# kv products of the second block on high and low parts of G and wv

## The chip, the core and the metric

One core of a Trainium2 chip runs the whole program. The metric is the device time of one execution in microseconds (us), the median of several runs. The core has a matrix engine (TensorE, PE in the profile, with its weight loads as PEld), three engines for element-wise work (VectorE or DVE, ScalarE or ACT, GpSimd or POOL) and SyncE (SP), which here only issues transfers. Each takes its instructions strictly in the order of the program. Matrix products read from SBUF and write to PSUM; the other engines take results out of PSUM.

## The reference

Two independent linear-attention blocks, A and B, on inputs of the same shape; the outputs stand side by side. For each of them, with S = 2048 tokens, D = 640, H = 32 heads of Dh = 20:

```python
qkv = (x @ wqkv).reshape(B, S, 3, H, Dh).transpose(2, 0, 3, 1, 4)
q, k, v = qkv[0], qkv[1], qkv[2]
phi = lambda t: jnp.where(t > 0, t + 1, jnp.exp(t)) + 1e-6
pq, pk = phi(q), phi(k)
kv = jnp.einsum("bhsd,bhse->bhde", pk, v)
z = jnp.einsum("bhsd->bhd", pk)
num = jnp.einsum("bhqd,bhde->bhqe", pq, kv)
den = jnp.einsum("bhqd,bhd->bhq", pq, z)[..., None] + 1e-6
o = num / den
out = o.transpose(0, 2, 1, 3).reshape(B, S, D) @ wo
```

All of it is float32.

## The kernel before

Large products aren't done in float32. Each operand is split into a high part, rounded to the type float32r (ScalarE copies, `ACTIVATE`), and a low part, the operand less the high part (VectorE, `TENSOR_TENSOR`), and three products high x high, high x low, low x high stand in for one (`mms`, `mm3`). In the second half of the kernel the helper `split` (lines 917 to 921) issues the ScalarE copy at once and only notes the subtraction in the list `lows`; `flush` issues what is noted, and `run` calls `flush` ahead of the work of its slot. So a low part stands on VectorE behind everything that was written between the `split` and the next slot.

v is never formed. With G = x^T phi(k), a 640 x 640 matrix, kv of a group of heads is wv^T G, cut to the heads' own blocks by a mask; then M = kv wo, folded over all heads, is one 640 x 640 matrix for each block, and the output is (phi(q) / den) M. The stages, in order of time:

- k stage: phi(k) for both blocks and G, summed up in five SBUF tiles `gacc` (one for each 128 rows c). A planner (`Plan`) orders this half by costs and due times. The last rounds of G of block B end it (psg, line 316; the sums on VectorE, line 537).
- q stages and output stages, written out by hand: q(0), q(1), out(0), q(2), out(1), ... up to out(7); u = 0 to 3 are tokens of block A, 4 to 7 of block B. A q stage (`qmm`) has five column pieces c, and for each five products k of three matrix instructions (lines 924 to 926), 512 columns wide, into the PSUM tile psq; then `qphi` takes psq through exp and relu on ScalarE (lines 1092, 1093) and one VectorE instruction (line 1094). psq rotates over three banks. An output stage (`outmm`) has 14 steps; ScalarE copies pa out (line 1249), VectorE adds pe and psb (line 1250).

Everything else is hung on slots: `at(("q", u, c, k), f, ...)` runs f right after product k of piece c of stage q(u), `at(("o", u, s), ...)` after step s of out(u). In the slots of q(0) stand the kv products of block B: `kvmm2(1, g)`, line 977, for six groups of heads g (four of 6 heads with 120 columns, two of 4 heads with 80), five products each over c, in float32: the 30 instructions show as 60 in the profile, each as two passes. The operands are `gacc[1, c]` and the loaded `wvt[1, g]`. Their slots are the pieces and products (0,2), (1,0), (1,3), (2,0), (2,3), (3,0).

Three more things around them matter later. `form_load` (line 1054) brings the split M of block A back from DRAM in ten pairs of transfers into tiles fh and fl; the first six have slots in q(0) and q(1), and go out on SyncE's queue. `load_xq` (line 957) brings the low parts xql of the next q stage, on the same queue, at ("q", 0, 3, 3) and ("q", 0, 4, 0) to ("q", 0, 4, 3). And `chain` (lines 1343 to 1365) spreads the sum over heads that makes the denominator (`fold1` to `fold5`, with ScalarE copies and VectorE sums) over the steps of the output stage before: for v = 1 they stand at steps 3, 4, 5, 6, 7, 9 and 11 of out(0).

Of the kernel before, what the change touches and what calls it, by code (L numbers as in the profile page):

```python
# [9 lines left out]
F32R = mybir.dt.float32r  # L10
# [4 lines left out]
H = 32  # L15
DH = 20
EPS = 1e-6
GROUPS = [(0, 6), (6, 6), (12, 6), (18, 6), (24, 4), (28, 4)]
# [200 lines left out]
def tile_linear_attn_pair(ctx: ExitStack, tc: tile.TileContext, ins, out: bass.AP):  # L219
    nc = tc.nc  # L220
    P = 128
    S, D = ins[0]["x"].shape
    NC = D // P
# [17 lines left out]
    kx, kg, q1a, q1b, q2, q3 = [], [], [], [], [], []  # L241
# [24 lines left out]
    gacc = {}  # L266
# [385 lines left out]
    wl, wh = ([Space(n, D, (XD,), F32R) for _ in range(NC)] for n in ("wkl", "wkh"))  # L652
# [16 lines left out]
    def whalf(h, *t):  # L669
        return [x[0][h * HF:h * HF + HF] for x in t]  # L670
# [6 lines left out]
    a, z, x = jh[0][0:P], jl[0][0:P], jr[0][0:P]  # L677
# [22 lines left out]
    for h in range(2):  # L700
        hi, lo = whalf(h, wh, wl)
# [79 lines left out]
    def filled(i, h, where=(1, 3, 4, 5, 6)):  # L781
        fill = {}
        for c, n in enumerate(where):
            fill.setdefault(n, []).append((gstep, i, h, c))
        return fill
# [9 lines left out]
    for p in range(4, NPB):  # L795
        i, h = divmod(p - 2, 2)
# [9 lines left out]
    for p in range(NPB + 1, NP):  # L806
        if p == NPB + 1:
            fl = kvs
        else:
            i, h = divmod(p - NPB - 2, 2)  # L810
            gready(NG + i)
            fl = filled(NG + i, h, *((LAST,) if p in (NPB + 2, NP - 1) else ()))
# [26 lines left out]
    wst, whl, wvt, xt, xts = {}, {}, {}, {}, {}  # L839
# [5 lines left out]
    def late(pool, name, cols, bufs):  # L845
        s = Late(name, cols, None, F32R)
        s.pool = pool
        s.make = lambda: s.open([P, cols], F32R, name=name, tag=name, bufs=bufs)
        return s

    for c in range(NC):
        hi, lo, raw = late(q1b, "wh", D, 5), late(q1b, "wl", D, 5), Space("wq", D, ANY)
# [13 lines left out]
    for c in range(NC):  # L866
        hi, lo, raw = late(q1b, "xqh", 512, 6), late(q1b, "xql", 512, 6), Space("xqs", 512, ANY)
# [13 lines left out]
    for g, (h0, nh) in enumerate(GROUPS):  # L881
        cols = NC * DH * nh
        w = Space("wv", cols, (BD,))
# [17 lines left out]
    def bank(name, tag="one", bufs=3):  # L901
        at, n = ptags[tag]
        pn[tag] = pn.get(tag, -1) + 1
        return psum.tile([P, 512], F32, name=name, tag=f"bank{at + pn[tag] % n}", bufs=1)

    def turned(tag, n):
        turn[tag] = (turn.get(tag, -1) + 1) % n
        return f"{tag}{places[turn[tag]] if tag == 'wst' else turn[tag]}"
# [3 lines left out]
    def flush():  # L912
        while lows:
            lo, src, hi = lows.pop(0)
            nc.vector.tensor_tensor(lo, src, f32(hi), op=OP.subtract)

    def split(hi, lo, src, now=False):
        nc.scalar.activation(hi, src, AF.Copy)  # L918
        lows.append((lo, src, hi))
        if now:  # L920
            flush()

    def mm3(o, whi, wlo, xhi, xlo, first, last):
        nc.tensor.matmul(o, whi, xhi, start=first, stop=False)  # L924
        nc.tensor.matmul(o, whi, xlo, start=False, stop=False)  # L925
        nc.tensor.matmul(o, wlo, xhi, start=False, stop=last)  # L926
# [3 lines left out]
    def at(slot, f, *a):  # L930
        todo.setdefault(slot, []).append((f, a))
# [34 lines left out]
    def load_o(b, g):  # L966
# [7 lines left out]
        nc.sync.dma_start(o, ins[b]["wo"][h0 * DH:(h0 + nh) * DH, :])  # L974
        wot[b, g] = o

    def kvmm2(b, g):
        h0, nh = GROUPS[g]
        r = DH * nh
        w = wvt.pop((b, g))  # L980
        ps = bank("pskv", "e", 2)
        for c in range(NC):
            gd = gacc[b, c].rearrange("p (d h) -> p d h", h=H)[:, :, h0:h0 + nh]
            nc.tensor.matmul(ps[:r, :r].rearrange("p (d h) -> p d h", h=nh), w[:, c, :], gd,
                             start=(c == 0), stop=(c == NC - 1))
        t = base.tile([r, r], F32, name="kvt", tag="kvt0", bufs=1)
        hi, lo = (base.tile([r, r], F32R, name=f"kv{t}", tag=turned("kvs", 12), bufs=1) for t in "hl")
        nc.vector.tensor_tensor(t, ps[:r, :r], mask[nh][:r, :], op=OP.mult)
        split(hi, lo, t)
        kvt[b, g] = (hi, lo)  # L990
# [79 lines left out]
    pq, acc, den, dd = {}, {}, {}, {}  # L1070
# [222 lines left out]
            at(s, form_store, b, i)  # L1293

    for i in range(6):
        at((("q", 0, 2, 1), ("q", 0, 2, 4), ("q", 0, 3, 1), ("q", 1, 0, 0), ("q", 1, 0, 2), ("q", 1, 1, 0))[i],
           form_load, 0, i)
    for i in range(6, 10):
        at(("q", 1, i - 5, 4) if i < 9 else ("q", 1, 4, 0), form_load, 0, i)

    for g in range(NGR):
        at(("q", 0, 0, 0), load_o, 1, g)
        at(("q", 0, (0, 1, 1, 2, 2, 3)[g], (2, 0, 3, 0, 3, 0)[g]), kvmm2, 1, g)
        at(("q", 0, 1 + g, 1) if g < 4 else ("q", 1, 0, 2 * g - 7), split_o, 1, g)
        at((("q", 0, 2, 2), ("q", 0, 3, 2), ("q", 0, 4, 4), ("q", 0, 4, 4), ("q", 1, 1, 2), ("q", 1, 2, 2))[g], mmm2, 1, g)
        at((("q", 0, 2, 4), ("q", 0, 3, 4), ("q", 1, 0, 1), ("q", 1, 0, 3), ("q", 1, 1, 4), ("q", 1, 2, 4))[g],
           store_m, nc.gpsimd)

    for c, a in ((0, ("q", 1, 4, 1)), (2, ("q", 1, 4, 1)), (4, ("q", 2, 0, 3)), (1, ("q", 4, 0, 2)), (3, ("q", 4, 0, 2))):
        at(a, load_w, "m", 1, c)  # L1310
    at(("o", 0, 5), form_sums1, 1, 0)
# [9 lines left out]
    h = NG - 1  # L1321
# [26 lines left out]
    for v in range(1, NU):  # L1348
        w, u = v - 1, v + 1
        if v == NU - 1:  # L1350
            chain[v] = [(("o", w, 1), split_acc, v), (("o", w, 4), denmm, v), (("o", w, 4), recip, v, 0),
                        (("o", w, 5), divide, v, 0), (("o", w, 6), a_split, v, 0, 0), (("o", w, 6), d_sums, v, 0, 0),
                        (("o", w, 7), d_split, v, 0, 0), (("o", w, 8), a_split, v, 1, 0), (("o", w, 8), d_sums, v, 1, 0),
                        (("o", w, 9), recip, v, 1), (("o", w, 10), d_split, v, 1, 0), (("o", w, 12), divide, v, 1),
                        (("o", v, 0), a_split, v, 0, 1), (("o", w, 13), d_sums, v, 0, 1),
                        (("o", v, 0), d_split, v, 0, 1), (("o", v, 2), d_sums, v, 1, 1),
                        (("o", v, 2), a_split, v, 1, 1), (("o", v, 3), d_split, v, 1, 1)]
        else:
            a = (3, 4, 5, 6, 7, 9, 11) if v == 1 else (2, 3, 5, 6, 7, 9, 11)
            chain[v] = [(("o", w, a[0]), fold1, v), (("o", w, a[1]), fold2, v), (("o", w, a[2]), fold3, v, 0),  # L1360
                        (("o", w, a[3]), fold3, v, 1), (("o", w, a[4]), fold4, v), (("o", w, a[5]), fold5, v, 0),
                        (("o", w, a[6]), fold5, v, 1), (("o", w, 11), divide, v, 0), (("o", w, 12), divide, v, 1),
                        (("q", u, 0, 2), d_sums, v, 0), (("q", u, 0, 4), a_split, v, 0), (("q", u, 1, 2), d_sums, v, 1),
                        (("q", u, 2, 1), d_split, v, 0), (("q", u, 3, 1), a_split, v, 1),
                        (("q", u, 3, 4), d_split, v, 1)]
# [66 lines left out]
```

## Time and profile before

| | before |
|---|---|
| median of 3 runs | 569.47 us (569.34 to 569.63) |
| the profiled execution | 570.12 us |
| its span on the core | 568.3 us |
| mean granted TensorE clock | 0.999 |
| busy: PE / PEld / DVE / ACT / POOL | 561.9 / 533.4 / 429.0 / 363.6 / 62.9 us |
| q(0) and q(1), with kv and M of block B | 287.49 to 333.47 us |
| out(0) | 333.47 to 351.09 us |
| moved by DMA | 117.64 MB, mean 207 GB/s |

The span is the time between the first and the last recorded instruction; the 1.8 us between it and the execution's time lie outside the program's instructions. Matrix instructions are pipelined: the recorded duration of one (0.39 us for 512 columns) is longer than the distance to the next (0.23 us), so distances between starts say what one costs. The time before an instruction that its engine stood idle is printed with what ended it. In views of stretches (windows) each engine has its busy time and number of instructions, then the TensorE clock that was granted, the share of the DMA engines and GB/s.

### The profile page before, as it was taken

What the parts mean: (1) busy time and instruction counts of PE and PEld (TensorE: products, weight loads), DVE (VectorE), ACT (ScalarE), POOL (GpSimd) and SP (SyncE); (2) the same over time, 40 slices, a digit from 0 to 9 for tenths busy, and PEclk for the clock granted to TensorE, in tenths of its full rate; (3) what the DMA queues carried; (4) which work ended last, traced back from release to release, by engine and by line L of the source; (5) the groups of instructions that cost most, each with busy time, mean ns of one, the idle gap of its engine ahead of it and who ended that gap; (6) DMA issues with size and microseconds to landing.
All of it is one profiled execution on the core that took longest, in us unless ns stands there. A gap on an engine that the chain in (4) does not pass through costs nothing. (4 is left out here: it accounts for less than half of the span.)

```text
span 568.3 us, 9523 instructions
## 1 busy us (share of the span) xinstructions
PE 561.9 (99%) x3512; PEld 533.4 (94%) x3512; DVE 429.0 (75%) x712; ACT 363.6 (64%) x673; POOL 62.9 (11%) x103
## 2 busy tenths in 40 slices
PE   8999999999999999999999999999999999999997
PEld 6999999999999999999988898898989989898997
DVE  6788677599888757988745798867788685767792
ACT  6778566574688756666446668675767666665551
POOL 0210111110001021110010103110012201001010
PEclk9999999999999999999999999999999999999999
DMA  8994664758849767696999975663373997122022
GB/s 292 358 293 122 177 167 104 243 150 236 273 122 265 197 169 197 190 295 202 340 294 337 357 255 175 250 229 120 101 247 119 349 389 264 47 76 92 1 93 92
DMA packets 68321, 117.64 MB, mean 207 GB/s; under 512 B 6804, under 2 KB 30132, under 8 KB 68276
## 3 DMA queue, kind: packets, MB, share of 16 engines
q1 hardware_dynamic: 59060, 89.94, 48.1%
q0 software_dynamic: 8928, 26.92, 17.1%
q8 instruction: 27, 0.44, 0.3%
q10 hardware_dynamic: 288, 0.20, 0.1%
q14 instruction: 18, 0.15, 0.1%
HBM read 71.13 MB, written 35.41 MB: 187 GB/s over the span
## 5 line engine op out<-in xcount | busy, mean ns | idle before, releaser
L316 PE MATMUL psg<-pkl,xnh 128*128 128x320 f32 x320 | 98.9, 309 | 0.0
L316 PE MATMUL psg<-pkh,xnh 128*128 128x320 f32 x320 | 98.8, 309 | 0.0
L316 PE MATMUL psg<-pkh,xnl 128*128 128x320 f32 x320 | 98.5, 308 | 0.0
L924 PE MATMUL psq<-xqh,wh 128*128 128x512 f32 x200 | 78.4, 392 | 0.0
L926 PE MATMUL psq<-xqh,wl 128*128 128x512 f32 x200 | 78.0, 390 | 0.0
L925 PE MATMUL psq<-xql,wh 128*128 128x512 f32 x200 | 77.9, 389 | 0.0
L489 ACT ACTIVATE kt<-ka 128x320 f32<-128x320 f32 x52 | 22.7, 437 | 59.1 <-PE ka L316 59.0
L316 PEld LDWEIGHTS psg<-pkl,xnh 128*128 128x128 f32 x320 | 60.1, 188 | 0.0
L316 PEld LDWEIGHTS psg<-pkh,xnl 128*128 128x128 f32 x320 | 60.1, 188 | 0.0
L316 PEld LDWEIGHTS psg<-pkh,xnh 128*128 128x128 f32 x320 | 60.0, 188 | 0.0
L406 POOL DMA_DIRECT2D zacc<-ek x32 | 26.5, 840 | 236.9 <-DVE ek L499 176.9
L1094 DVE SCALAR_TENSOR_TENSOR pq<-eq,rq 128x512 f32<-128x512 f32 x40 | 27.6, 691 | 32.1 <-ACT rq L1093 32.0
L1092 ACT ACTIVATE eq<-psq 128x512 f32<-128x512 f32 x40 | 23.9, 597 | 38.2 <-PE psq L926 35.9
L537 DVE TENSOR_TENSOR gacc<-psg,gacc 128x320 f32<-128x320 f32 x60 | 29.4, 490 | 23.7 <-PE psg L316 22.7
L926 PEld LDWEIGHTS psq<-xqh,wl 128*128 128x128 f32 x200 | 37.5, 188 | 7.9
L925 PEld LDWEIGHTS psq<-xql,wh 128*128 128x128 f32 x200 | 37.6, 188 | 7.3
L924 PEld LDWEIGHTS psq<-xqh,wh 128*128 128x128 f32 x200 | 37.6, 188 | 7.2
L1249 ACT ACTIVATE o<-pa 128x320 f32<-128x320 f32 x64 | 27.8, 437 | 25.6 <-PE pa L1234 25.1
L1234 PE MATMUL pa<-fh,dah 128*128 128x320 f32 x96 | 29.7, 310 | 1.4 <-ACT o L1249 1.4
L401 ACT ACTIVATE pkh<-ek,epst 128x640 fp32r<-128x640 f32 x32 | 26.5, 828 | 6.9 <-DVE ek L499 6.7
L1234 PE MATMUL pa<-fl,dah 128*128 128x320 f32 x96 | 29.7, 309 | 0.0
L1234 PE MATMUL pa<-fh,dal 128*128 128x320 f32 x96 | 29.6, 309 | 0.0
(222 smaller groups left out, 1564.4 us busy)
## 6 DMA issues: line engine op xcount, KB each, us to landing
zacc<-ek POOLq DMA_DIRECT2D x32, 320.0 KB, 4.8
xql<-xd SPq DMA_DIRECT2D x40, 256.0 KB, 4.9
xd<-xl SPq DMA_DIRECT2D x29, 320.0 KB, 4.3
out<-o POOLq DMA_DIRECT2D x28, 320.0 KB, 3.8
xns<-in_A_x SPq DMA_DIRECT2D x16, 320.0 KB, 5.5
xts<-in_B_xt_tiles SPq DMA_DIRECT2D x16, 320.0 KB, 3.7
xns<-in_B_x SPq DMA_DIRECT2D x16, 320.0 KB, 6.0
xqs<-in_A_xt SPq DMA_DIRECT2D x20, 256.0 KB, 5.6
```

Source lines behind the costliest of these rows:

```text
L316: nc.tensor.matmul(o, a.r, w.r, start=start and k == i == 0, stop=k == n - 1 and i == 2, skip_group_check=True)
L401: note("ACT", n + 110, lambda: act(hi.r, p.f, AF.Identity, bias=epst), [hi], [p, K0.all], by=8.0)
L406: note("POOL", 1.0, lambda: nc.gpsimd.dma_start(z.f, p.f, **kw), [z], [p], dma=1.0 if first else 1.86)
L489: note("ACT", HF, lambda: act(o.f, BK[k].tile[:, :HF], AF.Copy), [o], [BK[k].all])
L537: tt(o, BK[k].tile[:, :HF], o, op=OP.add)
L924: nc.tensor.matmul(o, whi, xhi, start=first, stop=False)
L925: nc.tensor.matmul(o, whi, xlo, start=False, stop=False)
L926: nc.tensor.matmul(o, wlo, xhi, start=False, stop=last)
L1092: nc.scalar.activation(e, ps, AF.Exp)
L1094: nc.vector.scalar_tensor_tensor(pq[u][:, c, :], e, 1.0, r, op0=OP.min, op1=OP.add)
L1234: nc.tensor.matmul(ps, x, y, start=start and n == i == 0, stop=n == len(terms) - 1 and i == 2, skip_group_check=True)
L1249: copy = lambda x, y: nc.scalar.activation(x, y, AF.Copy)
```

## The change

The kv products of block B get split operands. `gsplit(c)` makes a high part gh and a low part gl of `gacc[1, c]` (five of 640 columns), `vsplit(g)` a high part wvh and a low part wvl of the loaded wv of a group (four of 600 columns, two of 400). `kvmm2` then runs three float32r products in place of one float32 product: 90 instructions for 30. The new tiles lie in SBUF places of q tiles and of fh and fl that are free at that time, and the slots of `kvmm2` move back by two or three products, the first three `form_load`s move behind them, and the fold chain of v = 1 starts two steps later.

```diff
+    gs = {}
+
+    def gsplit(c):
+
+        if c == 0:
+            gs["all"] = q2[0].tile([P, NC, 512], F32R, name="gh", tag="pq", bufs=2).rearrange("p c s -> p (c s)")
+        g = gacc[1, c]
+        hi = gs["all"][:, c * D:c * D + D] if c < 4 else q2[0].tile([P, D], F32R, name="gh", tag="dah0", bufs=1)
+        lo = q1a[0].tile([P, D], F32R, name="gl", tag="fl", bufs=6)
+        split(hi, lo, g)
+        gs[c] = hi, lo
+
+    def vsplit(g):
+        w = wvt[1, g].rearrange("p c e -> p (c e)")
+        cols = NC * DH * GROUPS[g][1]
+        hi, lo = (q1a[0].tile([P, D], F32R, name=f"wv{t}", tag="fh", bufs=6)[:, :cols] for t in "hl")
+        split(hi, lo, w)
+        wvt[1, g] = [t.rearrange("p (c e) -> p c e", c=NC) for t in (hi, lo)]
+
     def kvmm2(b, g):
...
-        w = wvt.pop((b, g))
+        wh, wl = wvt.pop((b, g))
         ps = bank("pskv", "e", 2)
+        o = ps[:r, :r].rearrange("p (d h) -> p d h", h=nh)
         for c in range(NC):
-            gd = gacc[b, c].rearrange("p (d h) -> p d h", h=H)[:, :, h0:h0 + nh]
-            nc.tensor.matmul(ps[:r, :r].rearrange("p (d h) -> p d h", h=nh), w[:, c, :], gd,
-                             start=(c == 0), stop=(c == NC - 1))
+            gh, gl = (t.rearrange("p (d h) -> p d h", h=H)[:, :, h0:h0 + nh] for t in gs[c])
+            mm3(o, wh[:, c, :], wl[:, c, :], gh, gl, c == 0, c == NC - 1)
...
     for i in range(6):
-        at((("q", 0, 2, 1), ("q", 0, 2, 4), ("q", 0, 3, 1), ("q", 1, 0, 0), ("q", 1, 0, 2), ("q", 1, 1, 0))[i],
+        at((("q", 0, 3, 4), ("q", 0, 4, 1), ("q", 0, 4, 3), ("q", 1, 0, 0), ("q", 1, 0, 2), ("q", 1, 1, 0))[i],
            form_load, 0, i)
...
+    for c in range(NC):
+        at(("q", 0, 0, max(0, c - 1)), gsplit, c)
     for g in range(NGR):
         at(("q", 0, 0, 0), load_o, 1, g)
-        at(("q", 0, (0, 1, 1, 2, 2, 3)[g], (2, 0, 3, 0, 3, 0)[g]), kvmm2, 1, g)
+        at(("q", 0, (1, 1, 2, 2, 3, 3)[g], (0, 3, 0, 3, 0, 3)[g]), kvmm2, 1, g)
...
+    for g, a in enumerate((("q", 0, 0, 4), ("q", 0, 0, 4), ("q", 0, 0, 4), ("q", 0, 1, 3), ("q", 0, 2, 0), ("q", 0, 2, 3))):
+        at(a, vsplit, g)
...
-            a = (3, 4, 5, 6, 7, 9, 11) if v == 1 else (2, 3, 5, 6, 7, 9, 11)
+            a = (5, 6, 7, 7, 8, 10, 11) if v == 1 else (2, 3, 5, 6, 7, 9, 11)
```

Where the changed program puts these instructions shows in three places. The first is VectorE's list at the start of q(0). zsum, zturn and zp belong to the sums z over phi(k); kvt and kvl come out of a finished kv group, pq out of a finished column piece of q. Before:

```order
L602 STREAM_TRANSPOSE zturn<-zsum 128x640
L603 TENSOR_REDUCE zp<-zturn 128x5x4
L988 TENSOR_TENSOR kvt<-pskv,mask_74 120x120
L915 TENSOR_TENSOR kvl<-kvt,kvh 120x120
L1094 SCALAR_TENSOR_TENSOR pq<-eq,rq 128x512
```

And in the changed program:

```order
L602 STREAM_TRANSPOSE zturn<-zsum 128x640
L603 TENSOR_REDUCE zp<-zturn 128x5x4
L915 TENSOR_TENSOR gl<-gacc,gh 128x640 x5
L1113 SCALAR_TENSOR_TENSOR pq<-eq,rq 128x512
L915 TENSOR_TENSOR wvl<-wv,wvh 128x600 x3
L1007 TENSOR_TENSOR kvt<-pskv,mask_74 120x120
L915 TENSOR_TENSOR kvl<-kvt,kvh 120x120
```

All five gl and the first pq now stand ahead of the first wvl. On TensorE the first kv group follows the 18th matrix instruction of q(0) (before: the ninth), and its own third instruction reads that wvl:

```order
L924 MATMUL psq<-xqh,wh 128x512
L925 MATMUL psq<-xql,wh 128x512
L926 MATMUL psq<-xqh,wl 128x512
L924 MATMUL pskv<-gh,wvh 120x120
L925 MATMUL pskv<-gl,wvh 120x120
L926 MATMUL pskv<-gh,wvl 120x120
```

The second place is SyncE's list near the end of q(0): xqs and xql are the next stage's operands, fh and fl the pairs of `form_load`. Before:

```order
L955 DMA xqs<-in_A_xt 128x512 x4
L1068 DMA fh<-fdh_96 128x640
L1068 DMA fl<-fdl_97 128x640
L955 DMA xqs<-in_A_xt 128x512
L1068 DMA fh<-fdh_98 128x640
L1068 DMA fl<-fdl_99 128x640
L1068 DMA fh<-fdh_100 128x640
L1068 DMA fl<-fdl_101 128x640
L959 DMA xql<-xd_85 128x512 x5
```

And in the changed program:

```order
L955 DMA xqs<-in_A_xt 128x512 x5
L959 DMA xql<-xd_85 128x512
L1087 DMA fh<-fdh_96 128x640
L1087 DMA fl<-fdl_97 128x640
L959 DMA xql<-xd_85 128x512
L1087 DMA fh<-fdh_98 128x640
L1087 DMA fl<-fdl_99 128x640
L959 DMA xql<-xd_85 128x512 x2
L1087 DMA fh<-fdh_100 128x640
L1087 DMA fl<-fdl_101 128x640
L959 DMA xql<-xd_85 128x512
```

Two pairs of fh and fl now stand between the second and the last xql. The third place is ScalarE's list in out(0): o is the copy of pa out of PSUM, ac the fold chain's copies, xqh and fsh high parts of other operands. Before:

```order
L1249 ACTIVATE o<-pa 128x320 x2
L1126 ACTIVATE ac<-acc 64x256
L1127 ACTIVATE ac<-acc 64x256
L1249 ACTIVATE o<-pa 128x320
L962 ACTIVATE xqh<-xqs 128x512
L1249 ACTIVATE o<-pa 128x320
L1140 ACTIVATE ac<-ac 32x256 x2
L962 ACTIVATE xqh<-xqs 128x512
L1140 ACTIVATE ac<-ac 32x256 x2
L918 ACTIVATE fsh<-wst 128x640
L1249 ACTIVATE o<-pa 128x320
```

And in the changed program:

```order
L1268 ACTIVATE o<-pa 128x320 x3
L962 ACTIVATE xqh<-xqs 128x512
L1268 ACTIVATE o<-pa 128x320
L1145 ACTIVATE ac<-acc 64x256
L1146 ACTIVATE ac<-acc 64x256
L962 ACTIVATE xqh<-xqs 128x512
L918 ACTIVATE fsh<-wst 128x640
L1159 ACTIVATE ac<-ac 32x256 x4
L1268 ACTIVATE o<-pa 128x320
```

Four output copies come ahead of the first fold copy now, two before, and the four later fold copies stand in one row ahead of the fifth.

## The prediction

> **What bounds the kernel now.** The page's busy times come first:
>
> ```profile
> PE 561.9 (99%) x3512; PEld 533.4 (94%) x3512; DVE 429.0 (75%) x712; ACT 363.6 (64%) x673; POOL 62.9 (11%) x103
> ```
>
> TensorE is busy for 99% of the span. A busy TensorE need not be at its peak, so the stages that the change touches are read by stretches. The columns are the stretch and its length, then for PE, PEld, DVE, ACT and POOL the busy time with the number of instructions, then the granted TensorE clock, the DMA share and GB/s.
>
> ```profile
> 287.49:333.47 45.98, 45.98 (x250) 39.28 (x249) 31.17 (x51) 26.78 (x53) 6.42 (x11) 1.00 0.96 318
> 333.47:351.09 17.62, 16.25 (x110) 15.86 (x108) 16.03 (x25) 13.81 (x30) 2.57 (x5) 1.00 0.51 161
> 368.12:383.96 15.84, 15.84 (x109) 15.84 (x108) 10.68 (x17) 11.75 (x26) 3.03 (x6) 1.00 0.69 243
> ```
>
> The first stretch is q(0) and q(1), the second out(0), the third out(1). In the q stages TensorE never waits: what is added to its list, and each new wait, goes straight into the time. VectorE (31 of 46 us) and ScalarE (27) have room on average, which says nothing of one moment. out(0) has the same products as out(1) and takes 1.78 us more: that is the only time nearby that can be won back.
>
> **Term 1, the products: +2.8 us.** The timeline of TensorE and its weight loads around two kv groups (start, length, engine, line, count):
>
> ```profile
> 289.34 0.39 PE L926 MATMUL psq<-xqh,wl 128*128 128x512 f32 x1
> 289.57 1.21 PE L984 MATMUL pskv<-gacc,wv 128*120 128x120 f32 x10
> 290.51 0.19 PEld L924 LDWEIGHTS psq<-xqh,wh 128*128 128x128 f32 x1
> 290.54 0.47 PE L924 MATMUL psq<-xqh,wh 128*128 128x512 f32 x1
> 290.63 0.19 PEld L925 LDWEIGHTS psq<-xql,wh 128*128 128x128 f32 x1
> 290.86 0.39 PE L925 MATMUL psq<-xql,wh 128*128 128x512 f32 x1
> 302.30 0.88 PE L984 MATMUL pskv<-gacc,wv 128*80 128x80 f32 x10
> 302.95 0.19 PEld L924 LDWEIGHTS psq<-xqh,wh 128*128 128x128 f32 x1
> ```
>
> Five float32 products are ten passes. A weight load starts with the instruction ahead of its own, so the load at 290.51 marks the tenth pass: (290.51 - 289.57) / 9 = 0.104 us a pass at 120 columns, (302.95 - 302.30) / 9 = 0.072 at 80. That is the distance of weight loads too: the 128-column load of 290.51 lets the next one start at 290.63, and the instruction of 290.54 is followed only at 290.86, 0.32 us on, where 512 columns otherwise take 0.23. It stood until its weights were in. So a short product goes as fast as weights load, some 0.11 us for 128 columns, 0.104 for 120, 0.072 for 80. A float32r product loads as many weight columns and is one pass; no row shows one narrower than 320. Taken at the pace of the weights, a group has 15 in place of 10: 5 x 0.104 = 0.52 us, 5 x 0.072 = 0.36; 4 x 0.52 + 2 x 0.36 = **+2.8**. Bounds: 512 columns take 0.23 and 320 take 0.147,
>
> ```profile
> 343.87 0.31 PE L1234 MATMUL pa<-fl,dah 128*128 128x320 f32 x1
> 344.02 0.31 PE L1234 MATMUL pa<-fh,dal 128*128 128x320 f32 x1
> ```
>
> so 0.43 ns a column and a line through 0.06 us at 120 and 0.04 at 80: 15 x 0.06 = 0.9 in place of 1.04, and -0.5 for all six groups if columns alone counted. Above, a narrow float32r product at the price of both float32 passes, 0.21 and 0.14: 15 x 0.21 - 1.04 = 2.1, and 1.4, so +11.2. I stay with the weights, the nearest row.
>
> [...]
>
> **Term 2, a wait for the first wvl: +4.0 us.** VectorE's list at the start of q(0), and rows for what the change puts into it:
>
> ```profile
> 289.89 0.82 DVE L603 TENSOR_REDUCE zp<-zturn 128x20 f32<-128x640 f32 x1
> 281.06 1.55 DVE L861 TENSOR_TENSOR wl<-wq,wh 128x640 fp32r<-128x640 f32 x2
> 293.39 0.69 DVE L1094 SCALAR_TENSOR_TENSOR pq<-eq,rq 128x512 f32<-128x512 f32 x1 [1.63 <-ACT rq L1093]
> 294.00 0.28 DVE L988 TENSOR_TENSOR kvt<-pskv,mask 120x120 f32<-120x120 f32 x1
> 278.48 1.98 ACT L857 ACTIVATE wh<-wq 128x640 fp32r<-128x640 f32 x3
> 292.27 0.60 ACT L1092 ACTIVATE eq<-psq 128x512 f32<-128x512 f32 x1 [0.83 <-PE psq L926]
> 292.76 0.59 ACT L1093 ACTIVATE rq<-psq 128x512 f32<-128x512 f32 x1
> ```
>
> zp ends at 290.7. Then come five gl; wl is the same operation and size, two in 1.55 us, 0.73 apart: until 294.35. Then pq, which hands on after 0.61 (293.39 to 294.00): 294.96. Then the first wvl, 600 columns, 0.78: **295.75**, and the signal. ScalarE's part is no later: its gh start once the last G products have left the place that they take, about 287.6; five at 0.63 (wh: three in 1.98) and three wvh at 0.6 end near 292.6, then eq and rq until 293.7, ahead of pq's turn at 294.35. TensorE reaches the first kv group after 18 instructions of 0.23 us, 287.49 + 4.14 = 291.63, runs two products, and wants wvl at 291.84. It waits 295.8 - 291.84 = **4.0 us**. Queued behind is all of TensorE's list, which nothing reorders, so the wait is paid whole. The later wvl have three or more products of cover each, 2 us against 0.8, and cost nothing. Bounds: 3.4 if VectorE hands on faster, 4.6 if pq has to wait for rq; 0 only if that list were not in the way at all.
>
> **Term 3, the clock: +1.2 us.** Rows for what a wait does to TensorE's clock:
>
> ```profile
> 345.70 0.41 PE L1234 MATMUL pa<-fh,dah 128*128 128x320 f32 x1 [1.37 <-ACT o L1249]
> 564.49 0.31 PE L1234 MATMUL pe<-fh,dal 128*128 128x320 f32 x1
> 567.00:567.60 0.60, 0.00 (x0) 0.00 (x0) 0.00 (x0) 0.00 (x0) 0.00 (x0) 1.00 0.00 0
> 567.60:568.30 0.70, 0.00 (x0) 0.00 (x0) 0.00 (x0) 0.00 (x0) 0.00 (x0) 0.52 0.00 0
> L647 PE MATMUL psi<-idle 128*128 128x512 bf16 x10 | 4.0, 581 | 1.0 <-DVE ones L324 1.0
> ```
>
> The 1.4 us idle of 344 left the clock at 1.00 (stretch rows above). The last product starts at 564.49, and from 567.6, 3.1 us on, the clock is about half. A wait of 4.0 us is longer than that. At the start ten 512-column products take 4.0 us, 0.4 each against 0.23 later: after some 4 us of work the clock is up. If it falls about 3 us into the wait, one more microsecond of its up-time passes in the wait, and some 2.4 us of work go at half speed, which loses **1.2 us**. Bounds: 0, if it doesn't fall; 2.1, if it falls at the wait's end and 4.2 us go slowly.
>
> [...]
>
> **Term 4, xql behind the fh and fl pairs: +0.4 us.**
>
> ```profile
> 309.48 2.36 SPq L959 DMA_DIRECT2D xql<-xd  x4
> 316.97 0.39 PE L925 MATMUL psq<-xql,wh 128*128 128x512 f32 x1
> xql<-xd SPq DMA_DIRECT2D x40, 256.0 KB, 4.9
> 294.00:327.00 33.00, 33.00 (x182) 28.27 (x181) 20.67 (x35) 20.80 (x43) 5.84 (x10) 1.00 1.03 336
> ```
>
> The last four xql can't go out before TensorE has read the old ones, in the last column piece of q(0); they go 309.48 to 311.8, the last lands after 4.9 us at about 316.4, and q(1) wants it at 316.97. With two pairs between them, 1.28 MB more lie ahead of it, 3.8 us at 336 GB/s, less the 0.5 us of margin: +3.3 at worst. But the queue is emptier by then: the first pair, which now goes ahead of that point, has had 7 us (the added time) to land, and the old order had three pairs there. Nearer to nothing, I take 0.4; lower bound 0.
>
> **Term 5, the fold chain: -1.0 us.**
>
> ```profile
> 343.72 0.84 ACT L1140 ACTIVATE ac<-ac 32x256 f32<-32x256 f32 x2
> 344.58 0.74 ACT L918 ACTIVATE fsh<-wst 128x640 fp32r<-128x640 f32 x1
> 345.23 0.42 ACT L1249 ACTIVATE o<-pa 128x320 f32<-128x320 f32 x1
> ```
>
> TensorE's 1.4 us idle at 345.70 ends with the copy of 345.23, which stood behind two fold copies and fsh. In the new order four output copies come ahead of the fold chain, but four fold copies (4 x 0.33 = 1.3 us) then stand in a row before the fifth. Between all of the 1.78 and nothing I take -1.0.
>
> **No cost:** the added high and low parts, 11 on ScalarE (about 7.6 us by the rows above) and 11 on VectorE (8.3), lie beside TensorE's work after the first group; without that cover each would cost what term 2 shows. The form pairs are wanted in out(0), 16 us and more after their new slots.
>
> **Sum:** 2.8 + 4.0 + 1.2 + 0.4 - 1.0 = +7.4. The profiled execution took 570.12 us (span 568.3 and 1.8 around it) and would take 577.5; the median, 0.65 lower, goes from 569.47 to **576.9**.
>
> **Rivals.**
> - The clock stays up: term 3 is 0, 575.7. For it speaks that a wait of 4.0 us is not much over 3.1; against it the end of the trace. 30%.
> - Narrow float32r products cost both passes: term 1 is 11.2, 585.3. For it: no row shows one below 320 columns; against it: one pass for each wide one. 9%.
> - Narrow products go by columns: term 1 is -0.5, 573.6. Against it is the product held up for its weights at 290.54. 7%.
> - The wait is hidden, VectorE gets to wvl before TensorE: terms 2 and 3 are 0, 571.7. Against it is the order. 4%.
> - Not slower: the fold chain is the one mechanism with a minus sign. It can give back 1.78 us in out(0), and decides only where everything else comes to less; with no wait and products by columns the time is 569.47 - 0.5 + 0.4 - 1.78 = 567.6. Or the products aren't changed as said. 3%.
>
> **How the numbers follow.** The forecast has 47%. 573.3 to 578.6 takes in the first rival, the third, and the spread of terms 2 to 5 upward, and leaves out the second, the fourth and the last, 16%. About 0.2% (1.1 us) is what a measurement of this kernel can tell from no change: slower by more 96%, within it 2%, faster 2%.
>
> **What would show it.** Weight loads of pskv 0.104 and 0.072 us apart, 15 a group, bear out term 1. An idle of about 4 us ahead of a pskv product near 292, ended by VectorE's wvl, bears out term 2; none there overthrows it. A granted clock below 1.00 in the stretch 292 to 300, and psq products 0.46 us apart, bear out term 3. A psq wait for xql near 324 is term 4; out(0) at about 16.6 us is term 5. The forecast is wrong in kind if TensorE doesn't wait in q(0), or if pskv products lie 0.2 us apart.

## The result, and the profile after

| | before | after |
|---|---|---|
| median of 4 runs each | 569.40 us (569.09 to 569.63) | 584.43 us (583.60 to 585.33) |
| the profiled execution | 570.12 us | 583.60 us |
| its span, mean granted clock | 568.3 us, 0.999 | 581.8 us, 0.993 |
| q(0) and q(1) | 45.98 us | 60.51 us |
| out(0) | 17.62 us | 16.24 us |

The changed kernel is slower: 1.0256 times the time before [1.0244, 1.0268], +15.0 us where +7.4 was forecast. The profiled execution is the shortest of the four. Its span is 13.5 us longer: 14.5 in q(0) and q(1), -1.4 in out(0), and 0.35 ahead of q(0), where nothing is changed (over the twelve profiles here q(0) starts anywhere from 286.68 to 288.15 us); all later stages are equal within 0.01 us. The other three executions had a lower mean clock, 0.988 to 0.991; by estimate one further 3.41 us stretch of half clock, such as those below, lowers the mean by 0.003 (3.41 / 2 / 581.8) and costs up to 1.7 us.

The page of the changed kernel, its busy times, its clock row and one group:

```profile
PE 569.0 (98%) x3542; PEld 539.5 (93%) x3542; DVE 436.8 (75%) x723; ACT 370.4 (64%) x684; POOL 62.9 (11%) x103
PEclk9999999999999999999989899999999999999999
L925 PE MATMUL psq<-xql,wh 128*128 128x512 f32 x200 | 79.2, 396 | 4.1 <-DMA xql<-xd 4.1
```

TensorE is "busy" for 98%, and that tells nothing of 13 lost microseconds. The clock row does: two of 40 slices have fallen. So does the last column of the group: psq waited 4.1 us for xql, in a kernel whose q stages had no wait before.

The stretches, in the columns named with the table before. First q(0) and q(1), then out(0); then the 3.4 us ahead of the clock's first fall, the 3.4 us after it, and those after the second fall:

```profile
287.84:348.35 60.51, 52.63 (x280) 44.51 (x279) 40.64 (x64) 34.93 (x66) 6.42 (x11) 0.94 0.77 248
348.35:364.59 16.24, 16.12 (x110) 15.85 (x109) 13.13 (x21) 11.25 (x25) 2.14 (x4) 1.00 0.48 171
293.60:297.00 3.40, 0.91 (x9) 0.91 (x9) 3.40 (x6) 1.11 (x2) 2.14 (x4) 1.00 0.93 274
297.00:300.40 3.40, 3.40 (x13) 2.92 (x13) 1.81 (x4) 0.93 (x2) 0.08 (x1) 0.50 1.06 247
331.10:334.50 3.40, 3.40 (x9) 2.62 (x8) 0.86 (x2) 1.90 (x3) 0.00 (x0) 0.51 1.04 399
```

TensorE was idle for 60.51 - 52.63 = 7.9 us where it had no idle time, and 6.8 us of its work ran at half clock, which loses 3.4 more. Both places show in TensorE's timeline. Start, length, line, and in brackets the idle time with what ended it; first around the first kv group:

```profile
291.98 0.23 PE L924 MATMUL pskv<-gh,wvh 128*120 128x120 f32 x1
292.05 0.27 PE L925 MATMUL pskv<-gl,wvh 128*120 128x120 f32 x1
296.09 0.33 PE L926 MATMUL pskv<-gh,wvl 128*120 128x120 f32 x1 [3.77 <-DVE wvl L915]
296.25 0.27 PE L924 MATMUL pskv<-gh,wvh 128*120 128x120 f32 x1
...
296.88 0.28 PE L924 MATMUL pskv<-gh,wvh 128*120 128x120 f32 x1
...
297.55 0.40 PE L925 MATMUL pskv<-gl,wvh 128*120 128x120 f32 x1
297.75 0.40 PE L926 MATMUL pskv<-gh,wvl 128*120 128x120 f32 x1
297.95 0.74 PE L924 MATMUL psq<-xqh,wh 128*128 128x512 f32 x1
```

From 292.05 to 296.09 is 4.04 us where 0.10 would do: a wait of 3.94. Then products 0.105 us apart at full clock ((296.88 - 296.25) / 6), and 0.20 apart once it has fallen at 297.00. The second place is in q(1):

```profile
324.17 0.39 PE L924 MATMUL psq<-xqh,wh 128*128 128x512 f32 x1
325.23 0.50 PE L925 MATMUL psq<-xql,wh 128*128 128x512 f32 x1 [0.67 <-DMA xql<-xd]
...
326.49 0.40 PE L924 MATMUL psq<-xqh,wh 128*128 128x512 f32 x1
330.32 0.50 PE L925 MATMUL psq<-xql,wh 128*128 128x512 f32 x1 [3.43 <-DMA xql<-xd]
```

Against the usual 0.23 us the two waits are 0.83 and 3.60 us, 4.43 together. SyncE's list shows what the late xql stood behind, with the time at which each transfer was issued:

```profile
318.27 0.32 SPq L959 DMA_DIRECT2D xql<-xd  x1
318.64 0.54 SPq L1087 DMA_DIRECT2D fh<-fdh  x1
319.22 0.43 SPq L1087 DMA_DIRECT2D fl<-fdl  x1
319.76 1.10 SPq L959 DMA_DIRECT2D xql<-xd  x2
320.97 0.37 SPq L1087 DMA_DIRECT2D fh<-fdh  x1
321.39 0.42 SPq L1087 DMA_DIRECT2D fl<-fdl  x1
321.90 0.61 SPq L959 DMA_DIRECT2D xql<-xd  x1
```

Four fh and fl of 320 KB each, 1.31 MB, went out between the first and the last xql. Issuing them took little: the last xql was issued at 321.90. It was wanted at 326.72 (326.49 + 0.23), and the product that waited for it started at 330.32.

The added time then is: products 2.8 (measured below with no wait beside them), wait for wvl 3.94, first stretch of half clock 1.70, waits for xql 4.43, second stretch 1.70, which makes 14.6 against the 14.53 in q(0) and q(1). The experiments take these apart.

### The profile page after: what moved, and what is told of

Read it like the earlier page. It is cut to its first block, busy times and chain, and to the rows that moved or that the text cites. A ratio compares the mean times of both kernels' runs of the same rounds, so it can differ in the third digit from the quotient of the medians.

```text
span 581.8 us, 9610 instructions
## 1 busy us (share of the span) xinstructions
PE 569.0 (98%) x3542; PEld 539.5 (93%) x3542; DVE 436.8 (75%) x723; ACT 370.4 (64%) x684; POOL 62.9 (11%) x103
## 5 line engine op out<-in xcount | busy, mean ns | idle before, releaser
L925 PE MATMUL psq<-xql,wh 128*128 128x512 f32 x200 | 79.2, 396 | 4.1 <-DMA xql<-xd 4.1
```

## The experiments

The ratio behind a time is to the kernel before, run beside it, with its 95% interval in brackets.

### Without the xql wait (e1)

The changed kernel, with the second and third pair issued behind the last xql.

```diff
-        at((("q", 0, 3, 4), ("q", 0, 4, 1), ("q", 0, 4, 3), ("q", 1, 0, 0), ...)[i],
+        at((("q", 0, 3, 4), ("q", 0, 4, 4), ("q", 0, 4, 4), ("q", 1, 0, 0), ...)[i],
             form_load, 0, i)
```

> The changed kernel with the second and third pair of fh and fl moved behind the last xql (slot q 0,4,4). Place theory: the two TensorE waits for xql in q(1) (0.8 and 3.6 us) come from these two pairs standing ahead of the last xql on SyncE's queue; both waits go, and the second stretch of half clock (3.4 us, 1.7 us lost) goes with them: 584.4 - 4.4 - 1.7 = 578.3 us, 577.6 to 579.2. Rival, late theory: the waits come from all the transfers being out of step with a stage that starts 7 us late, wherever the pairs stand: 583.5 to 585.

Measured: 579.05 us (578.03 to 579.35), 1.0157 [1.0142, 1.0172], and no wait for xql in the profile. Two slots are worth 5.4 us. The stretches of this kernel: q(0) with q(1), and the time at half clock, of which TensorE worked from 296.40 on:

```profile
288.15:343.31 55.16, 51.38 (x281) 44.21 (x280) 38.88 (x62) 32.95 (x64) 6.44 (x11) 0.94 0.79 255
294.53:301.36 6.83, 4.96 (x19) 4.48 (x20) 4.56 (x8) 1.74 (x3) 2.23 (x4) 0.50 0.99 256
```

q(0) and q(1) are 5.35 us shorter than in the changed kernel: 4.43 and 1.70 of the second fall are gone, and the first fall came earlier here, at 294.53, 2.1 us into the wait, and lasted for 6.83 us, of which 4.96 were work: 2.5 lost in place of 1.7.

### The wait filled with work (e5)

The same kernel, with 15 products of the size of psq, whose result nobody reads, ahead of the first kv group.

```diff
         ps = bank("pskv", "e", 2)
+        if g == 0:
+            zw, zb = whl["q", 0, 0][0][:, :P], xt[0, 0][0]
+            pi = bank("psi", "e", 2)
+            for i in range(15):
+                nc.tensor.matmul(pi, zw, zb, start=True, stop=True)
```

> As e1, with 15 products of 512 columns (operands of q(0), result unused) ahead of the first kv group, 3.4 us of work in the time in which TensorE waits for the first wvl. Idle theory: the clock falls because TensorE idles for 4 us; filled, it stays up and 1.7 us are saved against e1: 576.6 us, mean clock 1.00 but for the start, no psq instructions 0.43 us apart near 298. Rival, narrow theory: the clock falls for the narrow products themselves: as e1, 578.3. If the filling is paid beside the wait: 580 and more.

Measured: 576.17 us (575.52 to 576.42), 1.0108 [1.0091, 1.0124]. TensorE's timeline and the span with the mean clock:

```profile
core 0: 574.3 us, clock 1.000
```

```profile
291.61 3.57 PE L1004 MATMUL psi<-xqh,wh 128*128 128x512 f32 x15
295.02 0.23 PE L924 MATMUL pskv<-gh,wvh 128*120 128x120 f32 x1
295.08 0.27 PE L925 MATMUL pskv<-gl,wvh 128*120 128x120 f32 x1
295.73 0.33 PE L926 MATMUL pskv<-gh,wvl 128*120 128x120 f32 x1 [0.38 <-DVE wvl L915]
295.89 0.28 PE L924 MATMUL pskv<-gh,wvh 128*120 128x120 f32 x1
```

The 15 products took 3.41 us, wvl came no sooner (a wait of 0.55 is left, 3.96 in all), and yet the kernel is 2.9 us faster than without them: the clock never fell, and q(0) with q(1) are 2.33 us shorter, close to the 2.5 us that half speed had cost (the rest of the 2.9 lies ahead of q(0), where nothing differs). So it was the idle time that dropped the clock here (0.50 from 294.53 on without the filling, 1.000 in the mean with it), and not the narrow products.

### The old fold steps (e4)

The first experiment's kernel, with the fold chain at its old steps.

```diff
-            a = (5, 6, 7, 7, 8, 10, 11) if v == 1 else (2, 3, 5, 6, 7, 9, 11)
+            a = (3, 4, 5, 6, 7, 9, 11) if v == 1 else (2, 3, 5, 6, 7, 9, 11)
```

> As e1, with the fold chain of v = 1 back at its old steps. Theory: the 1.4 us that out(0) won come from these steps, so they are lost again: 578.3 + 1.4 = 579.7 us, out(0) 17.6 us long. Rival: out(0) is shorter since q(0) and q(1) end later and other engines have caught up: 578.3, out(0) 16.2 us.

Measured: 578.69 us (577.88 to 579.59), 1.0154 [1.0139, 1.0169]: no longer than the kernel with the new steps, where 1.4 us more were expected; the medians don't tell the two apart. The profiles do: out(0) takes 17.63 us here, as before the change, and 16.77 with the new steps. In these two profiles the new steps bring 0.86 us in that stage.

### The products alone (e6)

The changed kernel with its kv groups six products later (the expectation miscounts them as four or five), the splits of the last three groups and the work that follows from the groups moved along, and all pairs behind the last xql.

```diff
-        at(("q", 0, (1, 1, 2, 2, 3, 3)[g], (0, 3, 0, 3, 0, 3)[g]), kvmm2, 1, g)
+        at(("q", 0, (2, 2, 3, 3, 4, 4)[g], (1, 4, 1, 4, 1, 4)[g]), kvmm2, 1, g)
...
-        at((("q", 0, 3, 4), ("q", 0, 4, 1), ("q", 0, 4, 3), ("q", 1, 0, 0), ("q", 1, 0, 2), ("q", 1, 1, 0))[i],
+        at((("q", 1, 0, 0), ("q", 1, 0, 0), ("q", 1, 0, 1), ("q", 1, 0, 2), ("q", 1, 0, 3), ("q", 1, 1, 0))[i],
```

> The changed kernel with the kv groups four or five products later (slots 2,1 to 4,4), what follows them moved along, and all fh and fl pairs behind xql. Theory: no wait for wvl, no fall of the clock, no wait for xql; left are 2.8 us of narrow products less 1.4 us in out(0): 569.4 + 1.4 = 570.8 us, 570.2 to 571.6. Rival: the added high and low parts on ScalarE and VectorE (16 us of work in q(0)) aren't covered wherever the groups stand: 573 or more.

Measured: 572.12 us (571.49 to 572.83), 1.0038 [1.0025, 1.0051], 0.5 us above the upper end of what was expected: out(0) won 0.8 us and not 1.4. No wait for wvl or xql and no fall of the clock is in the profile; out(0) is 16.81 us:

```profile
287.16:336.31 49.15, 49.12 (x280) 42.07 (x279) 38.07 (x62) 32.56 (x65) 6.42 (x11) 1.00 0.87 273
```

q(0) and q(1) are 3.17 us longer than before. By the distances between starts the six kv groups take 8.17 us where they took 5.24, and all psq products together 34.69 in place of 34.83: +2.8. The products of M are 0.3 longer, which wasn't followed further, and the two products of the denominator (psd) 0.1.

### Twice the columns (e7)

The kernel of the products alone, with kv products of 240 and 160 columns in place of 120 and 80 (twice the heads of G; the mask takes out the group's own half).

```diff
-        o = ps[:r, :r].rearrange("p (d h) -> p d h", h=nh)
+        ha = h0 - nh if g in (3, 5) else h0
+        o = ps[:r, :2 * r].rearrange("p (d h) -> p d h", h=2 * nh)
...
-            gh, gl = (t.rearrange("p (d h) -> p d h", h=H)[:, :, h0:h0 + nh] for t in gs[c])
+            gh, gl = (t.rearrange("p (d h) -> p d h", h=H)[:, :, ha:ha + 2 * nh] for t in gs[c])
...
```

> As e6, with each kv product 240 or 160 columns wide in place of 120 or 80 (the neighbouring heads' columns are computed too and left unused). Weight theory: a narrow product takes the time of its weight load (0.104 us for 120 weight columns, 0.072 for 80), so twice the moving columns fit almost beneath it: distances 0.11 and 0.08 us, e6 + 0.9 us at most. Column theory: the time goes with the moving columns (0.87 ns each): distances 0.21 and 0.14 us, e6 + 8 us.

Measured: 573.40 us (573.08 to 573.78), 1.0066 [1.0053, 1.0080], 1.3 us above the kernel of the products alone, where 0.9 was the most expected. The first of the 15 products of a group and the psq behind the last, for the first, the second and the fifth group:

```profile
295.11 0.28 PE L924 MATMUL pskv<-gh,wvh 128*120 128x240 f32 x1
...
296.81 0.39 PE L924 MATMUL psq<-xqh,wh 128*128 128x512 f32 x1
...
298.89 0.31 PE L924 MATMUL pskv<-gh,wvh 128*120 128x240 f32 x1
...
301.04 0.40 PE L924 MATMUL psq<-xqh,wh 128*128 128x512 f32 x1
...
311.07 0.24 PE L924 MATMUL pskv<-gh,wvh 128*80 128x160 f32 x1
...
312.20 0.43 PE L924 MATMUL psq<-xqh,wh 128*128 128x512 f32 x1
```

(296.81 - 295.11) / 15 = 0.113 us a product at 240 columns, 0.104 with half of them; the third and fourth group go at this pace too. (312.20 - 311.07) / 15 = 0.075 at 160 columns, 0.072 with half of them. So 160 columns on 80 weight columns went faster (0.075) than 120 on 120 (0.104): in these products it was the weights that set the pace, and neither the moving columns nor a fixed price of a product. The second group took (301.04 - 298.89) / 15 = 0.143, which is not explained; it makes 0.6 of the 1.08 us by which q(0) and q(1) are longer here. At the 0.23 us of 512 columns, 240 come to 0.108 (an estimate), so beyond this width the columns would no longer be free.

### The new pair slots alone (e2)

The kernel before, with the first three pairs at the changed kernel's slots; kv products and fold steps as before.

```diff
-        at((("q", 0, 2, 1), ("q", 0, 2, 4), ("q", 0, 3, 1), ("q", 1, 0, 0), ("q", 1, 0, 2), ("q", 1, 1, 0))[i],
+        at((("q", 0, 3, 4), ("q", 0, 4, 1), ("q", 0, 4, 3), ("q", 1, 0, 0), ("q", 1, 0, 2), ("q", 1, 1, 0))[i],
```

> The kernel before with nothing but the slots of the first three fh and fl pairs taken from the changed one. Place theory: two pairs stand between the second and the last xql here too, so q(1) waits for xql some 4 us, and the clock may fall for it: 573.5 to 575.5 us. Late theory: in step as before, no wait: 569.4 us.

Measured: 572.76 us (571.30 to 575.32, six runs), 1.0064 [1.0045, 1.0083], below the 573.5 to 575.5 expected. Three of the six had a mean clock of 0.999 or 1.000, the profiled one of 571.75 among them, and took 571.3 to 572.2; the other three had 0.994 to 0.997 and took 573.3 to 575.3. So the clock probably fell in these, but no profile shows it. In the table of waits (engine, line, what was waited for: us in all, times, the longest) stands what was not there before:

```profile
PE psq L925 <- DMA xql<-xd: 3.2, 2, 2.7
```

By the distances the waits are 0.68 and 2.84 us, and q(0) with q(1) are 49.58 us, 3.6 longer. So the slots alone make most of the wait, with none of the new products about. out(0) is 16.10 us here, with the old fold steps, 1.5 shorter than before. That VectorE and ScalarE catch up while TensorE waits in q(1), and part of the wait is won back there, is the likely reason; it wasn't taken apart.

### Half the bytes ahead of xql (e9)

The kernel of the last experiment, with the second and third pair brought in two halves, the second halves behind the last xql.

```diff
+        parts = [*zip(fd.pop((b, i)), r)]
+        if b == 0 and i in (1, 2):
+            for d, t in parts:
+                nc.sync.dma_start(f32(t)[:, :HF], d[:, :HF])
+            at(("q", 0, 4, 4), form_rest, parts)
+            return
...
```

> The kernel before with the changed slots of the first three pairs, and the second and third pair brought in two halves, the second halves behind the last xql: as many transfers stand between the xql, with half the bytes. Byte theory: the 3.5 us that q(1) waits for xql are the time of 1.3 MB; half of that is saved, 1.2 to 1.9 us of waiting are left, 570.4 to 571.3 us. Issue theory: what counts is the number of transfers that SyncE issues ahead of the last xql: 3.5 us or more, 572.8.

Measured: 570.57 us (569.99 to 570.91, ten runs), 1.0010 [1.0001, 1.0019].

```profile
PE psq L925 <- DMA xql<-xd: 1.4, 2, 0.8
```

By the distances 0.93 and 0.80, together 1.73 us, with as many transfers ahead of xql and half the bytes: 3.5 us of wait at 1.31 MB, 1.7 at 0.66 MB, none in the profile of before at 0. In these profiles, one of each kernel, the price goes by bytes, some 2.7 us for a megabyte, and not by the number of transfers issued.

### The new fold steps alone (e3)

The kernel before with the new fold steps.

```diff
-            a = (3, 4, 5, 6, 7, 9, 11) if v == 1 else (2, 3, 5, 6, 7, 9, 11)
+            a = (5, 6, 7, 7, 8, 10, 11) if v == 1 else (2, 3, 5, 6, 7, 9, 11)
```

> The kernel before with nothing but the new steps of the fold chain of v = 1. Theory: out(0) gets 1.4 us shorter, 569.4 - 1.4 = 568.0 us, ratio 0.9975. Rival: the gain in out(0) needs the later end of q(1): 569.4 us, ratio 1.000.

Measured: 568.98 us (568.31 to 570.33, eleven runs), 0.9992 [0.9984, 1.0001]: not told from no change, and a microsecond above the 568.0 expected. Its profile, of the longest of the eleven, has out(0) at 16.23 us, 1.4 shorter, and a wait for xql in q(1) that takes 1.19 of it:

```profile
315.19 0.39 PE L924 MATMUL psq<-xqh,wh 128*128 128x512 f32 x1
316.61 0.50 PE L925 MATMUL psq<-xql,wh 128*128 128x512 f32 x1 [1.03 <-DMA xql<-xd]
```

No pair stands between the xql there. The margin of before is so thin that an execution can wait for xql with the transfers in their old order.

### New fold steps, and all pairs behind xql (e8, e10)

The kernel before with the new fold steps of the last experiment, and with the first pairs behind the last xql.

```diff
-        at((("q", 0, 2, 1), ("q", 0, 2, 4), ("q", 0, 3, 1), ("q", 1, 0, 0), ("q", 1, 0, 2), ("q", 1, 1, 0))[i],
+        at((("q", 1, 0, 0), ("q", 1, 0, 0), ("q", 1, 0, 1), ("q", 1, 0, 2), ("q", 1, 0, 3), ("q", 1, 1, 0))[i],
```

> The kernel before with the new steps of the fold chain and with all fh and fl pairs behind the last xql (slots q 1,0,0 to 1,1,0). Theory: TensorE's 1.4 us in out(0) go, and xql no longer comes late in some executions (1.2 us in the profile of the run with the new fold steps alone): 568.0 us, 567.7 to 568.4, every run within 0.5 us. Rival: the pairs, wanted in out(0), come late themselves or xql does still: 569 to 570.

Measured: 570.21 us (568.41 to 572.91, twelve runs), 1.0004 [0.9993, 1.0015]: no gain, where 568.0 was expected. The profiled execution was the shortest, 568.41, with no wait for xql and out(0) at 16.78 us; 0.8 of its lead on the profile of before lies ahead of q(0). The same kernel was profiled once more to see a longer one:

> The kernel of e8 once more, for a second profile: its executions ran from 568.4 to 572.9 us, and the first profile is of the shortest. If xql still comes late in some of them, this profile shows a psq wait of 1 us or more in q(1) and out(0) below 16.8 us; if the fh and fl pairs come late, the wait stands at the first pa or pe products of out(0). If it shows neither, 568.4 to 569.0 us again.

It took 569.60 us, with out(0) at 17.55 and q(1) without a wait for xql, which is none of the cases that were expected. VectorE and ScalarE in that stage, of the second profile:

```profile
340.23 0.49 DVE L1021 TENSOR_TENSOR t<-wst 128x320 f32<-128x320 f32 x1 [0.72 <-DMA wst<-md]
```

```profile
343.00 1.69 ACT L1140 ACTIVATE ac<-ac 32x256 f32<-32x256 f32 x4 [0.97 <-DVE ac L1134]
344.71 0.44 ACT L1249 ACTIVATE o<-pa 128x320 f32<-128x320 f32 x1
```

and ScalarE at the same place in the first:

```profile
341.83 1.70 ACT L1140 ACTIVATE ac<-ac 32x256 f32<-32x256 f32 x4 [0.51 <-DVE ac L1134]
343.55 0.44 ACT L1249 ACTIVATE o<-pa 128x320 f32<-128x320 f32 x1
```

VectorE waited for wst, a part of M that comes back from DRAM; its sums of the fold chain stand behind that, the four fold copies behind the sums, and the output copy that TensorE waits for behind the copies. So the gain of the new fold steps hangs on when one transfer lands: about 0.85 us in one execution, 0.07 in the other. Whether the longer ones of the twelve were held up in the same way isn't known; the longest, 572.91, is the only one with a mean clock below 0.999 (0.996), which speaks for a fall of the clock.

## Why the prediction was right in kind and wrong in size

The direction, the two places of idle time and their causes were named beforehand; the time, 584.43, lies above the range. Step by step, for the profiled execution:

| step | forecast | measured | from |
|---|---|---|---|
| 1 products | +2.8 | +2.8 | distances between starts, in the kernel of the products alone |
| 2 wait for the first wvl | +4.0 | +3.94 | the 296.09 row |
| 3 clock after it | +1.2 | +1.70 | 3.41 us of work at 0.50 |
| 4 xql behind the pairs | +0.4 | +4.43 | the 325.23 and 330.32 rows |
| a second fall of the clock | not there | +1.70 | 3.41 us of work at 0.51 |
| 5 out(0) | -1.0 | -1.38 | the stretch rows |

**Step 1 held.** 0.104 us a product, 15 in a group, paced by weight loads: the doubled columns bear it out (0.113, where pace by columns alone would have doubled it), and the rivals "both passes" (0.21) and "by columns" (0.06) fell. "Both passes" gave 585.3 us, within 0.9 of the time measured; that is chance, its mechanism is in no row.

**Step 2 held**, and so did its working along VectorE's list:

```profile
290.25 0.82 DVE L603 TENSOR_REDUCE zp<-zturn 128x20 f32<-128x640 f32 x1
290.98 3.76 DVE L915 TENSOR_TENSOR gl<-gacc,gh 128x640 fp32r<-128x640 f32 x5
294.66 0.68 DVE L1113 SCALAR_TENSOR_TENSOR pq<-eq,rq 128x512 f32<-128x512 f32 x1
295.26 2.16 DVE L915 TENSOR_TENSOR wvl<-wv,wvh 128x600 fp32r<-128x600 f32 x3
```

zp, five gl, one pq, then the first wvl: 295.75 was forecast for its end, and with q(0) starting 0.35 us later the product went at 296.09.

**Step 3 was right in mechanism, a little small.** The clock did fall, as the filled wait shows, but at 297.00, after the wait and not in it, so that the whole 3.4 us at half speed were work: 1.70, inside the bounds of 0 to 2.1. (The 2.4 us of slow work in the forecast don't follow from its rows: some 4 us until the clock is up, less 1 in the wait, are 3, or 1.5 lost. The 4 us are the slow pace of the first ten products; the granted clock of the stretch from 0.00 to 4.40 us reads 1.00 before the change, so these rows don't show how long a low clock lasts. In the changed kernel it lasted 3.41 us.) "The clock stays up" fell.

**Step 4 is the step that failed**: +0.4 where 4.43 was measured, and with it the second fall of the clock, 1.70, that the sum has no term for. The mechanism was written down and the worst case worked out as +3.3; then the text went on "But the queue is emptier by then", and "Nearer to nothing, I take 0.4". The queue was emptier, but earlier. The DMA in q(0), in the columns of the stretches, in the changed kernel:

```profile
303.00:318.00 15.00, 15.00 (x107) 13.41 (x106) 8.91 (x19) 7.82 (x19) 1.25 (x2) 1.00 0.40 127
318.30:330.30 12.00, 7.92 (x38) 6.13 (x36) 6.39 (x12) 8.24 (x16) 1.20 (x2) 1.00 0.91 309
```

and for the 15 us ahead of the last four xql and the 12 us from them on, before:

```profile
294.50:309.50 15.00, 15.00 (x95) 13.14 (x94) 7.55 (x16) 8.15 (x19) 3.46 (x6) 1.00 1.03 314
309.50:321.50 12.00, 12.00 (x60) 10.05 (x59) 7.34 (x14) 9.17 (x19) 1.20 (x2) 1.00 1.00 342
```

Ahead of the point at which the xql may go out, the DMA moved 127 GB/s in place of 314. A part of what had been moved in that time had gone earlier, while TensorE waited for wvl and worked at half clock (259 GB/s from 287.84 to 303.00); but two pairs, 1.31 MB, now had to be moved after that point, between the xql. An idle queue earlier is of no use to a transfer that may not start yet. The worst case of 3.3 was the right estimate for the slots by themselves, 3.5 measured; half the bytes, 1.7. In the changed kernel the wait was 4.43, above that bound too. What the 0.9 us more are made of stays open.

**The missing step.** Had step 4 been taken at its own upper bound, 3.3, the reading of step 3 (the clock falls about 3 us into an idle time, taken from the end of the trace before the change, where it fell 3.1 us after the last product's start) would have applied to it too, and the sum would have been 2.8 + 4.0 + 1.2 + 3.3 + 1.2 - 1.0 = +11.5, still 2.0 short of the profiled +13.5: the wait and the two falls each came out above their terms. The forecast priced the clock once, for the wait it believed in. The two slots together, wait and second fall, are 6.1 us of the profiled +13.5; taking them away gained 5.4 in the median.

**Step 5 came out near the forecast, but not by the forecast's cause alone.** Where TensorE doesn't wait for xql, the new fold steps are worth 0.86 us in one pair of profiles, 0.85 and 0.07 in two others; with a wait for xql, out(0) is 1.5 shorter with the old steps too. In the changed kernel both are there, and the stage is 1.4 shorter.

**No cost** held for the added high and low parts: in the kernel of the products alone, where nothing waits for them, q(0) and q(1) are 3.17 us longer, and 2.8 of these are the kv products.

None of the kernels beat the one before by more than its interval: the new fold steps by themselves, 0.9992 [0.9984, 1.0001], come nearest.

## What to carry to other kernels

When a change moves transfers, count the bytes that stand between a transfer's earliest start and the moment it is wanted, and divide by the rate that the profile shows at that place; a queue that was emptier before that start (127 GB/s in place of 314) helped nothing here. Price an idle time on TensorE like the ones here (3.77 us ahead of the first wvl, 3.43 ahead of the last xql) twice, once as idle and once as work at half clock that may follow it (1.70 us lost each time), and fill it with products nobody reads where it can't be avoided: 15 of them won 2.3 us of q(0) and q(1) here. A product with few columns cost here what its weights took to load (0.104 us at 120 weight columns, 0.072 at 80), so three products in place of one float32 product of two passes took half as much again (8.17 us for the six groups in place of 5.24), at 120 and at 80 columns alike.

## What the runs showed of the hardware

The clock fell here after stretches that were not idle throughout. In the changed kernel it fell at 297.00, though TensorE had worked for 0.91 of the 3.40 us before (the row of that stretch above). Without the xql wait it fell 2.2 us after the last start, at 294.53, and 1.49 of the 3.41 us before were work:

```profile
291.12:294.53 3.41, 1.49 (x8) 1.11 (x6) 3.41 (x6) 3.08 (x6) 0.58 (x1) 1.00 0.67 179
```

So a quarter to over two fifths of these stretches was work. In the profile of the new pair slots alone, with a mean clock of 1.000, a wait of 2.84 us, 2.67 of them idle, didn't bring it down. The times at half clock were 3.41 us long, or twice that: 3.41 (297.00 to 300.41) and 3.41 (331.09 to 334.50) in the changed kernel, 6.83 (294.53 to 301.36) without the xql wait. What sets their length and the moment of a fall isn't shown.

The first product after the wait for wvl was slower to hand on than later ones: 0.16 us from 296.09 to the next start, and from 295.73 in the kernel with the filled wait, where later ones took 0.104.
